# Second attention of a fused attention and GELU network: six more exps added on VectorE, GpSimd's squares regrouped, the last roots of batch 2 computed from SBUF

## The chip, the cores and the metric

The program runs on one core of one Trainium2 chip. The metric is the device time of one execution in microseconds (us), taken as the median of several executions. Five engines work beside each other, each on its own queue, in the order in which its instructions stand: PE (matrix products, TensorE), DVE (VectorE), ACT (ScalarE), POOL (GpSimd) and SP, which only issues transfers. An instruction that waits holds back everything behind it on its engine.

## What is computed

The reference is an attention over 8 batches and 12 heads (448 positions, 64 wide) with a root-mean-square norm on q and k, and a two-layer network on its result:

```python
def rmsnorm(x, g):
    rms = np.sqrt(np.mean(x * x, axis=-1, keepdims=True) + 1e-06)
    return x / rms * g
q_n, k_n = (rmsnorm(q, g_q), rmsnorm(k, g_k))
scores = scale * np.matmul(q_n, k_n.transpose(0, 1, 3, 2))
attn = np.exp(scores - max) / sum
x = attn @ v            # then regrouped to 3584 tokens x 768
h = x @ w_in            # 768 x 2048
out = gelu_tanh(h) @ w_out
```

## The kernel before

**Groups and batches.** The 12 heads of a batch are three groups of four, called c0, c1 and c2; (2, c1) means batch 2, group 1. Batch b runs in two stretches. In its *attention*, PE makes 21 score tiles ("units" u0 to u20, seven for each group, line 335); ACT takes the exp of each (line 343); then come for each group a product of the exps with a block of ones, which gives the sums (s0, s1, s2), and one with v (x0, x1, x2, both line 387). In its *first layer* (line 537) PE multiplies the result with `win`, and ACT applies GELU (line 543). The second layer of earlier batches (line 495) is cut in small rounds and put between the units of an attention. Batch 0 and the last second layer have code of their own.

**What sets the order.** Each attention has two strings: one for PE ("5r" is five rounds of the second layer, "u" a unit, "s" and "x" the two products) and one for DVE. The attention of batch 1 uses `SECOND`, those of batches 2 to 7 use `STEADY`. DVE's letters are: A, B, F, G add the seven exp tiles of a group (lines 355 to 362), so that the ones product needs few matmuls; T, R, S turn, invert and spread the sums (lines 397, 402, 409); M multiplies the x product with them into `xT` (line 422); E evicts a second-layer tile. Letters L, J, K and a0, a1, ... are places at which other work hangs. `added(b, c)` tells how many exps are added: a sum product over seven exp tiles is 7 x 4 matmuls, over one added tile 4.

**Preparing the next batch.** While batch 1 runs, batch 2 is prepared: q and k are loaded (SP), squared (ACT or POOL, line 164), summed over 64 columns (DVE, `total`, line 173), the inverse roots are made (ACT with Ln and Exp, line 198 and 205, or DVE with three Newton steps, `rsqrt_last`, lines 254 to 262), POOL multiplies (`normed`, line 278), SP transposes by DMA into `qT` and `kT` (line 319), and DVE multiplies `kT` with the gains (`gain`, line 325). A raw buffer is one of four per tag: the load of (3, c2) takes the buffer of (2, c1), so it goes out when POOL has normed (2, c1). On SP the first layer of batch 1 issues: the transposes of (2, c0), the loads of (3, c1), the transposes of (2, c1), the loads of (3, c2), the transposes of (2, c2). POOL then squares (3, c2), and DVE takes its two totals and the gain of (2, c2) at the start of the attention of batch 2, ahead of A0, its first addition.

**PSUM.** Four tiles of two banks (t0 to t3) go round: `pair(...)` gives the one that was given longest ago, whatever for, and its new writer waits for the old reader.

Of the kernel before, what the change touches and what calls it, by code (L numbers as in the profile page):

```python
# [8 lines left out]
F32 = mybir.dt.float32  # L9
# [8 lines left out]
def kernel(  # L18
# [224 lines left out]
    def rsqrt_last(b):  # L243


        c, flat, m = slice(NCH - 1, NCH), "p c n a t -> p (c n a t)", 4 * NT
        y, ms = rinvs[b][:, c].rearrange(flat), sss[b][:, c].rearrange(flat)
        if steady():
            own, dst = pair("root")[:, 0], y
        else:  # L250
            own, dst = oall[0][:, S:], place(b, 1)
        z, u = own[:, :m], own[:, m:2 * m]
        t = smp.tile([P, NCH * 4 * NT], F32, tag="lg", name="lg")[:, :m]
        nc.vector.tensor_scalar(u, ms, 1.0 / D, 1e-6, op0=ALU.mult, op1=ALU.add)
        nc.vector.tensor_scalar(
            y.bitcast(I32), u.bitcast(I32), -0.5, float(0x5F3759DF), op0=ALU.mult, op1=ALU.add
        )
        for i in range(3):
            nc.vector.tensor_copy(z, y)
            nc.vector.tensor_mul(t, z, y)  # L260
            nc.vector.scalar_tensor_tensor(z, t, -0.5, u, op0=ALU.mult, op1=ALU.mult)
# [85 lines left out]
    def added(b, c):  # L347

        return NT - 1 if b > 1 else (NT - 1, 0, NT - 2)[c] if b else 0
# [21 lines left out]
    def products(b, c, what, lo=0, hi=NT):  # L371
# [8 lines left out]
        if not what and added(b, c):  # L380
            es[:added(b, c) + 1] = [ess[b, c][:, 0]]
# [166 lines left out]
    def mm1_pair(i, cs=range(HP), b=0, js=range(2)):  # L548
# [29 lines left out]
        "3r u 5r uu 8r u 8r uu 8r u 5r u 4r u 7r us 4r u 4r u 3r uu 4r x 1r usu 3r u 6r u 2r u 5r"  # L578
        " uu 10r x 6r sx",
        "A0 L0 B0 F0 G0 J0 T0 R0 K0 S0 a0 a1 M0 T1 R1 S1 a2 A2 a3 B2 F2 M1 a4 a5 T2 R2 S2 M2",  # L580
        {6: 0, 14: 1, 21: 2},
    )

    def attention(b, side, extra, ends):
# [65 lines left out]
        for word in order.split():  # L650
# [5 lines left out]
            for w in word:  # L656
# [7 lines left out]
                else:  # L664
                    last = added(b, k)
                    assert {("u", t) for t in range(k * NT, (k + 1) * NT)} <= made
                    assert w == "x" or not last or ("FG"[last - NT + 2], k) in made
# [257 lines left out]
    for b in range(B):  # L925
        m1, side, extra, ends = [], [], [], []
        if b == 0:
# [85 lines left out]
        if b + 2 < B:  # L1013
            ends.append(lambda: rsqrt(b + 2, slice(0, NCH if b else NCH - 1)))
# [41 lines left out]
```

## Time and profile before

| | us |
|---|---|
| median of 3 executions | 391.45 (391.40 to 391.76) |
| the profiled execution | 391.23 |
| its span, first to last instruction | 389.2 |
| granted TensorE clock | 1.000 |
| attention of batch 1 on PE | 50.0 to 75.7 |
| first layer of batch 1 on PE | 75.7 to 94.35 |
| start of the attention of batch 2 | 94.35 |

A row of a timeline has the start in us from the start of the span, the time from the first start to the last end, engine, line, operation, out<-in and how many instructions; in brackets stands the idle time ahead of it and what ended it. Starts of rows are exact; a matmul's end is modelled, so the pace of PE is read from one row's start to the next.

### The profile page before, as it was taken

The page shows a single profiled execution, that of the slowest core. Times are in us where ns is not written, and L with a number is a line of the kernel's source. Part 1 is how long each engine was busy: PE and PEld are TensorE (multiplying, and loading weights), DVE is VectorE, ACT ScalarE, POOL GpSimd, SP SyncE. Part 2 cuts the span into 40 slices and gives each one's busy share as a digit, 9 for nine tenths or more (in the row PEclk, how much of TensorE's full clock was granted, in tenths as well). Part 3 has the DMA queues.
Part 4 walks back from the last instruction along what each step waited for, and adds up shares of the span by engine and source line. Part 5 has one row for each costly group of instructions (what it writes and reads, how often), then busy time and mean ns, then how long its engine had stood idle before and what let it go on. Part 6 is the DMA issues. An engine that isn't in the chain of part 4 may idle for free.

```text
span 389.2 us, 17542 instructions
## 1 busy us (share of the span) xinstructions
PE 380.6 (98%) x8060; PEld 294.0 (76%) x8060; DVE 235.9 (61%) x366; ACT 278.7 (72%) x353; POOL 126.3 (32%) x110
## 2 busy tenths in 40 slices
PE   7899999999999999999999999999999999999996
PEld 4565577877887788877888788877888778887664
DVE  5998938976596359836589257953598204980010
ACT  6995499767994689757995589946897449944300
POOL 5996506384005440093103740064300900000000
PEclk9999999999999999999999999999999999999999
DMA  8999999999614992379822995159631721120033
GB/s 266 322 231 211 210 230 263 223 200 264 113 44 100 243 213 58 80 132 217 194 65 65 214 227 103 45 110 251 108 80 50 125 44 42 44 65 4 2 83 81
DMA packets 64446, 54.68 MB, mean 141 GB/s; under 512 B 37620, under 2 KB 60020, under 8 KB 64372
## 3 DMA queue, kind: packets, MB, share of 16 engines
q1 hardware_dynamic: 53936, 41.33, 43.8%
q0 software_dynamic: 10128, 11.80, 18.5%
q8 instruction: 63, 1.03, 1.1%
q10 hardware_dynamic: 308, 0.43, 0.4%
q14 instruction: 11, 0.09, 0.1%
HBM read 45.61 MB, written 11.01 MB: 146 GB/s over the span
## 4 chain that ended last, share of the span: by engine, by line
PE 92%; ACT 5%; DMA 1%; issue 1%; DVE 0%; POOL 0%; DVEq 0%
PE t L537 33%; PE t L495 32%; PE t L387 9%; PE t L335 7%; PE t L463 5%; ACT ex L343 4%; PE t L556 4%; DMA rawq<-in_q_dram 1%; PE h L436 1%; PE tp L296 1%; PE o L387 0%; POOL nrmq L278 0%; ACT g L543 0%; DVE ss L173 0%; ACT sq L162 0%
## 5 line engine op out<-in xcount | busy, mean ns | idle before, releaser
L343 ACT ACTIVATE ex<-t,shift 128x896 bf16<-128x896 f32 x168 | 156.2, 1016 | 1.9 <-PE t L335 1.6
L495 PE MATMUL t<-wout,g 64*64 64x384 bf16 (+1 forms) x3456 | 150.6, 305 | 0.0
L537 PE MATMUL t<-xT,win 64*64 64x448 bf16 x2688 | 128.7, 349 | 0.3 <-ACT g L543 0.3
L495 PEld LDWEIGHTS <-g 64*64 64x64 bf16 x3456 | 112.9, 107 | 19.2
L537 PEld LDWEIGHTS <-win 64*64 64x64 bf16 x2688 | 96.6, 107 | 31.0 <-issue 0.5
L543 ACT ACTIVATE g<-t 128x896 bf16<-128x896 f32 x56 | 50.5, 915 | 57.1 <-PE t L537 57.1
L173 DVE TENSOR_REDUCE ss<-sq 128x14 f32<-128x896 f32 (+3 forms) x45 | 44.5, 997 | 51.9 <-ACT sq L162 49.1
L335 PE MATMUL t<-qT,kT 64*64 64x448 bf16 x672 | 58.2, 351 | 1.4 <-ACT ex L343 0.6
L799 POOL COPY mark<-es 1x1 bf16<-1x1 bf16 x7 | 1.2, 177 | 132.0 <-DVE es L362 128.3
L355 DVE TENSOR_TENSOR es<-ex 128x1792 bf16<-128x1792 bf16 x20 | 21.2, 1061 | 33.0 <-ACT ex L343 33.0
L278 POOL TENSOR_TENSOR nrmq<-rawq,rinv 128x896 bf16<-128x896 f32 (+1 forms) x21 | 34.9, 1660 | 18.6 <-ACT rinv L205 11.0
L278 POOL TENSOR_TENSOR nrmk<-rawk,rinv 128x896 bf16<-128x896 f32 (+1 forms) x21 | 34.4, 1640 | 0.0
L387 PE MATMUL t<-ex,vb 64*64 64x448 bf16 x588 | 31.9, 350 | 0.0
L335 PEld LDWEIGHTS <-kT 64*64 64x64 bf16 x672 | 25.5, 106 | 7.3 <-DVE kT L305 1.2
L397 DVE STREAM_TRANSPOSE st<-t 128x448 f32<-128x448 f32 x42 | 24.7, 626 | 9.7 <-PE t L387 9.7
L387 PEld LDWEIGHTS <-vb 64*64 64x64 bf16 x672 | 23.5, 107 | 7.3 <-issue 1.0
L409 DVE STREAM_TRANSPOSE rb<-rc 128x896 f32<-128x896 f32 (+1 forms) x25 | 26.7, 1068 | 0.3
L705 DVE COPY osb<-t 128x384 f32<-128x384 f32 (+1 forms) x4 | 2.0, 507 | 35.2 <-PE t L463 35.2
L422 DVE TENSOR_TENSOR xT<-t,rb 128x896 bf16<-128x896 f32 x21 | 22.8, 1087 | 0.8
L164 POOL TENSOR_TENSOR sq<-rawq 128x896 f32<-128x896 f32 (+1 forms) x9 | 13.6, 1513 | 28.6 <-DVE ss L173 27.3
L513 ACT COPY osb<-t 128x768 f32<-128x768 f32 (+1 forms) x18 | 12.6, 701 | 13.9 <-PE t L495 13.9
L358 DVE TENSOR_TENSOR es<-es,ex 128x1792 bf16<-128x1792 bf16 x20 | 21.3, 1063 | 0.7 <-ACT ex L343 0.6
(103 smaller groups left out, 313.5 us busy)
## 6 DMA issues: line engine op xcount, KB each, us to landing
rawq<-in_q_dram SPq DMA_DIRECT2D x22, 448.0 KB, 5.0
rawk<-in_k_dram SPq DMA_DIRECT2D x22, 448.0 KB, 5.8
out_dram<-osb SPq DMA_DIRECT2D x42, 192.0 KB, 2.7
vb<-in_v_dram POOLq DMA_DIRECT2D x6, 672.0 KB, 7.3
win<-in_moe_w_in_dram POOLq DMA_DIRECT2D x8, 384.0 KB, 10.8
wout<-in_moe_w_out_dram POOLq DMA_DIRECT2D x3, 768.0 KB, 17.1
out_dram<-osb SPq DMA_DIRECT2D x24, 96.0 KB, 3.7
vb<-in_v_dram POOLq DMA_DIRECT2D x2, 448.0 KB, 15.5
```

The lines of the kernel that those rows point to most:

```text
L173: nc.vector.reduce_sum(sss[b][:, seat(b, c), "qk".index(n), hs, ts], squares(b, c, n, hs, ts), axis=AX.X)
L278: eng.tensor_mul(nrms[n, b, c][:, ts].rearrange("p t a d -> p a t d"), raws[n, b, c][:, :, ts], root[:, :, ts].to_broadcast([P, 2, m, D]),)
L335: nc.tensor.matmul(sc[r * R:(r + 1) * R, a, :S], kT[rs, c, t, r], qT[b][rs, c, :, r], start=True, stop=True,)
L343: nc.scalar.activation(exs[b, c][:, t], scs.pop((b, c, t))[:, :, :S], AF.Exp, scale=scale, bias=shift)
L358: nc.vector.tensor_add(es, es, ex[:, 4:6])
L387: nc.tensor.matmul(o[r][a * D:(a + 1) * D], vb[b % 2][rs, 2 * c + a, i] if what else ones[rs], es[i][rs, a], start=(i == 0), stop=(i == n ...
L397: nc.vector.transpose(st[:, r].rearrange("p a b -> p (a b)"), o[r])
L409: nc.vector.transpose(oas["rb"][:, rs].rearrange("p r s -> p (r s)"), rc.to_broadcast([128, (rs.stop - rs.start) * m, 32]),)
L422: nc.vector.tensor_mul(xT[b][:, 2 * c:2 * c + 2], oas["o", c, 1][:, :, :S], oas["rb"])
L495: mm = nc.tensor.matmul(o[a * R:(a + 1) * R, bank, :hi - lo], g[rs, f, at:at + R], wout[rs, f, lo:hi], start=(n == 0), stop=(n == len(step ...
L537: mm = nc.tensor.matmul(h[a * R:(a + 1) * R, j, :S], win[rs, c, at:at + R], xT[b][rs, c], start=begin and c == cs[0], stop=end and c == cs ...
L543: nc.scalar.activation(g[:, 2 * i:2 * i + 2, (b % 2) * S:(b % 2 + 1) * S], h[:, :, :S], AF.Gelu_apprx_tanh,)
```

## The change

The line numbers in the diff's new code are not those of the profile. Parts of the diff that only rename are left out.

```diff
-    def rsqrt_last(b):
+    def rsqrt_last(b, c=slice(NCH - 1, NCH)):
-        c, flat, m = slice(NCH - 1, NCH), "p c n a t -> p (c n a t)", 4 * NT
+        flat, m = "p c n a t -> p (c n a t)", (c.stop - c.start) * 4 * NT
         y, ms = rinvs[b][:, c].rearrange(flat), sss[b][:, c].rearrange(flat)
         if steady():
-            own, dst = pair("root")[:, 0], y
+            own = consts.tile([P, 2, m], F32, name="zu")
+            z, u = own[:, 0], own[:, 1]
+            dst = y
...
     def added(b, c):
-        return NT - 1 if b > 1 else (NT - 1, 0, NT - 2)[c] if b else 0
+        return NT - 1 if b > 1 else (NT - 1, NT - 2, NT - 2)[c] if b else 0
...
         if not what and added(b, c):
-            es[:added(b, c) + 1] = [ess[b, c][:, 0]]
+            es[:added(b, c) + 1] = [ess[b, c][:, i] for i in range(1 + ((b, c) == (1, 1)))]
...
     SECOND = (
-        "3r u 5r uu 8r u 8r uu 8r u 5r u 4r u 7r us 4r u 4r u 3r uu 4r x 1r usu 3r u 6r u 2r u 5r"
-        " uu 10r x 6r sx",
-        "A0 L0 B0 F0 G0 J0 T0 R0 K0 S0 a0 a1 M0 T1 R1 S1 a2 A2 a3 B2 F2 M1 a4 a5 T2 R2 S2 M2",
-        {6: 0, 14: 1, 21: 2},
+        "5r u 1r u 2r u 6r u 9r u 1r u 5r u 6r u 8r u 5r su 3r u 6r u 4r u 3r uxu 5r u 4r"
+        " us 1r u 6r uu 2r u 9r x 5r sx",
+        "A0 L0 B0 F0 G0 J0 T0 R0 S0 A1 K0 B1 M0 a0 T1 R1 A2 S1 B2 F2 M1 a1 T2 R2 S2 M2",
+        {8: 0, 13: 1, 21: 2},
     )
...
-                      ("L0", lambda: late_loads(2, 1)), ("a1", lambda: late_loads(2, 2)),
+                      ("L0", lambda: late_loads(2, 1)), ("a0", lambda: late_loads(2, 2)),
...
-            extra += [("J0", lambda: gpsimd_waits(ess[1, 0][:1, 0, 0, :1])),
-                      ("K0", lambda: gpsimd_waits(kT[:1, 2, 0, 0, :1]))]
-            at = 0
-            for c in range(2):
-                for n in "qk":
-                    for hs in (slice(0, 1), slice(1, 2)) if c else (both,):
-                        extra += [
-                            ("K0" if at else "J0",
-                             lambda c=c, n=n, hs=hs: square(2, c, n, nc.gpsimd, hs)),
-                            (f"a{at}", lambda c=c, n=n, hs=hs: total(2, c, n, hs))]
-                        at += 1
+            extra.append(("J0", lambda: gpsimd_waits(ess[1, 0][:1, 0, 0, :1])))
+            for at, n in enumerate("qk"):
+                extra += [
+                    ("J0", lambda n=n: square(2, 0, n, nc.gpsimd)),
+                    (f"a{at}", lambda n=n: total(2, 0, n))]
         elif b + 1 < B:
             m1.append((0, lambda: gpsimd_waits(ess[b, NCH - 1][:1, 0, 0, :1])))
+            if b == 1:
+                halves = [(n, slice(a, a + 1)) for n in "qk" for a in range(2)]
+                m1 += [(0, lambda n=n, hs=hs: square(2, 1, n, nc.gpsimd, hs)) for n, hs in halves]
+                m1 += [(0, lambda n=n, hs=hs: total(2, 1, n, hs)) for n, hs in halves]
+                m1 += [(0, lambda n=n: total(2, 2, n)) for n in "qk"]
+                m1.append((0, lambda: rsqrt_last(2, slice(1, NCH))))
             for c in range(NCH):
-                if b == 1 and c + 1 == NCH:
-                    m1 += [(0, lambda: total(2, 2, "q")), (0, lambda: total(2, 2, "k")),
-                           (0, lambda: rsqrt_last(2))]
                 m1 += [(0, lambda c=c: normed_both(b + 1, c, nc.gpsimd)),
                        (4 * c + 4, lambda c=c: transposed(b + 1, c))]
-            m1 += [(9, lambda: gain(b + 1, 0)), (14, lambda: gain(b + 1, 1))]
+            m1.append((9, lambda: gain(b + 1, 0)))
+            if b == 1:
+                extra.append(("first", lambda: gain(2, 1)))
+            else:
+                m1.append((14, lambda: gain(b + 1, 1)))
...
-            ends.append(lambda: rsqrt(b + 2, slice(0, NCH if b else NCH - 1)))
+            ends.append(lambda: rsqrt(b + 2, slice(0, NCH if b else 1)))
```

So the exps of (1, c1) are added by A1 and B1 into two half sums, and s1 is 3 x 4 matmuls in place of 7 x 4. POOL squares (2, c0) in one go in the attention of batch 1, and (2, c1) after it. ACT makes the roots of (2, c0) alone; DVE's Newton steps make those of (2, c1) and (2, c2) together, 56 columns in place of 28, and take no PSUM tile.

How the instructions stand on DVE from M1 of batch 1 (xT, the first row) to the Newton steps, before and then now. `ss<-sq` are totals, 128x7 a half and 128x14 a whole one; the rows from L397 (now L398) on are T2, R2, S2, M2.

```order
L422 TENSOR_TENSOR xT<-t_100,rb 128x896
L173 TENSOR_REDUCE ss<-sq 128x7 x2
L397 STREAM_TRANSPOSE st<-t_893 128x448 x2
L402 RECIPROCAL rc<-st 128x28
L409 STREAM_TRANSPOSE rb<-rc 128x896
L422 TENSOR_TENSOR xT<-t_101,rb 128x896
L173 TENSOR_REDUCE ss<-sq 128x14 x2
L254 TENSOR_SCALAR t_101<-ss 128x28
L255 TENSOR_SCALAR rinv<-t_101 128x28
```

```order
L423 TENSOR_TENSOR xT<-t_101,rb 128x896
L173 TENSOR_REDUCE ss<-sq 128x14
L398 STREAM_TRANSPOSE st<-t_893 128x448 x2
L403 RECIPROCAL rc<-st 128x28
L410 STREAM_TRANSPOSE rb<-rc 128x896
L423 TENSOR_TENSOR xT<-t_100,rb 128x896
L173 TENSOR_REDUCE ss<-sq 128x7 x4
L173 TENSOR_REDUCE ss<-sq 128x14 x2
L255 TENSOR_SCALAR zu<-ss 128x56
L256 TENSOR_SCALAR rinv<-zu 128x56
```

The four half totals of (2, c1) now stand between M2 and the Newton steps, and one whole total in place of two halves stands between M1 and T2.

POOL over the same stretch, before and then now. `mark` is a copy of one element by which POOL waits for an addition on DVE (or for `kT`), `sq` are squares (128x896 a whole group, 128x448 half a group), `nrmq` and `nrmk` the norming of (2, c0), (2, c1) and (2, c2) in this order.

```order
L799 COPY mark<-es 1x1
L164 TENSOR_TENSOR sq<-rawq 128x896
L799 COPY mark<-kT 1x1
L164 TENSOR_TENSOR sq<-rawk 128x896
L164 TENSOR_TENSOR sq<-rawq 128x448 x2
L164 TENSOR_TENSOR sq<-rawk 128x448 x2
L147 DMA vb_121<-in_v_dram 128x6x448
L799 COPY mark<-es 1x1
L278 TENSOR_TENSOR nrmq<-rawq,rinv 128x2x7x64
L278 TENSOR_TENSOR nrmk<-rawk,rinv 128x2x7x64
```

```order
L801 COPY mark<-es 1x1
L164 TENSOR_TENSOR sq<-rawq 128x896
L164 TENSOR_TENSOR sq<-rawk 128x896
L147 DMA vb_121<-in_v_dram 128x6x448
L801 COPY mark<-es 1x1
L164 TENSOR_TENSOR sq<-rawq 128x448 x2
L164 TENSOR_TENSOR sq<-rawk 128x448 x2
L279 TENSOR_TENSOR nrmq<-rawq,rinv 128x2x7x64
L279 TENSOR_TENSOR nrmk<-rawk,rinv 128x2x7x64
```

The squares of (2, c1) moved behind the second mark, that is behind F2 of batch 1, and stand ahead of the first norming. Behind these rows the order on POOL is as before, and so is DVE's from the totals of batch 3 to A0 of batch 2:

```order
L173 TENSOR_REDUCE ss_1831<-sq_1942 128x14
L173 TENSOR_REDUCE ss_1831<-sq_1971 128x14
L326 TENSOR_SCALAR kT_124<-kT_124,gcols_113 128x896
L173 TENSOR_REDUCE ss_1831<-sq_2052 128x14
L173 TENSOR_REDUCE ss_1831<-sq_2054 128x14
L326 TENSOR_SCALAR kT_124<-kT_124,gcols_113 128x896
L356 TENSOR_TENSOR es_2210<-ex_2112 128x1792
L514 COPY osb_2249<-t1_101 128x768
```

These are (now, with the numbers of the buffers) the two totals of (3, c1), the gain of (2, c1), the two totals of (3, c2), the gain of (2, c2), then A0 and the eviction E0; none of them moved against the others. On SP, the eight stores of the first two evictions now stand together ahead of the loads of (2, c2), and the transposes and loads behind them are in the order of before.

More of the change, by code (lines that the diff above doesn't have):

```diff
@@ L241, in rsqrt_newton @@
             )
-    def rsqrt_last(b):
-        c, flat, m = slice(NCH - 1, NCH), "p c n a t -> p (c n a t)", 4 * NT
+    def rsqrt_last(b, c=slice(NCH - 1, NCH)):
+        flat, m = "p c n a t -> p (c n a t)", (c.stop - c.start) * 4 * NT
         y, ms = rinvs[b][:, c].rearrange(flat), sss[b][:, c].rearrange(flat)
         if steady():
-            own, dst = pair("root")[:, 0], y
-        else:
-            own, dst = oall[0][:, S:], place(b, 1)
-        z, u = own[:, :m], own[:, m:2 * m]
+            own = consts.tile([P, 2, m], F32, name="zu")
+            z, u = own[:, 0], own[:, 1]
+            dst = y
+        else:
+            z, u = oall[0][:, S:S + m], oall[0][:, S + m:S + 2 * m]
+            dst = place(b, 1)
         t = smp.tile([P, NCH * 4 * NT], F32, tag="lg", name="lg")[:, :m]
@@ L666, in attention @@
                     assert {("u", t) for t in range(k * NT, (k + 1) * NT)} <= made
-                    assert w == "x" or not last or ("FG"[last - NT + 2], k) in made
+                    assert w == "x" or not last or ("BG" if (b, k) == (1, 1) else "FG")[
+                        last - NT + 2] + str(k) in {x + str(i) for x, i in made}
                     products(b, k, "sx".index(w))
```

## The prediction

> **What bounds the kernel now.** I read the page's chain of waits first, then PE's timeline over the stretch that the change touches, then the other engines' timelines there.
>
> ```profile
> PE 92%; ACT 5%; DMA 1%; issue 1%; DVE 0%; POOL 0%; DVEq 0%
> ```
>
> PE makes 92% of the chain that ended last, so the time changes only by matmuls that go and by time in which PE stands. From the timeline of PE (attention of batch 1, its first layer, attention of batch 2):
>
> ```profile
> 65.05 1.52 PE L387 MATMUL t<-ex,ones 64*64 64x448 bf16 x28
> 75.73 6.63 PE L537 MATMUL t<-xT,win 64*64 64x448 bf16 x136
> 82.62 11.92 PE L537 MATMUL t<-xT,win 64*64 64x448 bf16 x248 [0.26 <-ACT g L543]
> 94.35 1.01 PE L495 MATMUL t<-wout,g 64*64 64x384 bf16 x20
> 102.66 0.39 PE L335 MATMUL t<-qT,kT 64*64 64x448 bf16 x4
> ```
>
> The 248 matmuls of the third row take 94.35 - 82.62 = 11.73 us. Four 64x64 ones run side by side, so that is 62 groups of 0.19 us. The 136 of the second row, 34 groups, should take 6.43 and take 82.62 - 75.73 = 6.89: PE stands 0.46 us there, and waits for ACT's GELU. The last row is u7 of batch 2. It needs the PSUM tile that E0 empties on DVE. From DVE's timeline (end of batch 1's attention, its first layer, start of batch 2's attention):
>
> ```profile
> 73.30 1.09 DVE L422 TENSOR_TENSOR xT<-t,rb 128x896 bf16<-128x896 f32 x1
> 74.31 1.14 DVE L173 TENSOR_REDUCE ss<-sq 128x7 f32<-128x448 f32 x2
> 75.36 1.17 DVE L397 STREAM_TRANSPOSE st<-t 128x448 f32<-128x448 f32 x2
> 78.17 1.09 DVE L422 TENSOR_TENSOR xT<-t,rb 128x896 bf16<-128x896 f32 x1
> 79.18 2.07 DVE L173 TENSOR_REDUCE ss<-sq 128x14 f32<-128x896 f32 x2
> 81.28 0.19 DVE L254 TENSOR_SCALAR t<-ss 128x28 f32<-128x28 f32 x1
> 95.55 1.08 DVE L173 TENSOR_REDUCE ss<-sq 128x14 f32<-128x896 f32 x1 [0.58 <-POOL sq L164]
> 96.55 0.44 DVE L325 TENSOR_SCALAR kT<-kT,gcols 128x896 bf16<-128x896 bf16 x1
> 100.56 1.09 DVE L355 TENSOR_TENSOR es<-ex 128x1792 bf16<-128x1792 bf16 x1 [3.56 <-ACT ex L343]
> 101.57 0.95 DVE L513 COPY osb<-t 128x768 f32<-128x768 f32 x1
> ```
>
> A0 of batch 2 starts at 100.56 and E0 ends at 102.52, 0.14 us ahead of u7. So PE goes straight through, but with next to nothing to spare. What covers it is the 3.56 us for which DVE had been idle before A0: the last total of batch 3 (95.55) and the last gain of batch 2 (96.55) were done early. That cover is what the change spends.
>
> **What goes.** s1 has 12 matmuls in place of 28: 4 groups of 0.19 less, 0.76 us. The Newton steps no longer take one of the four PSUM tiles in turn, so the fourth GELU pair gets the tile that M2 has freed, not the one whose GELU has just begun: the 0.46 us go. With nothing else PE would be 1.22 us earlier at the attention of batch 2. The two extra additions A1, B1 (about 1 us each on DVE) lie beside PE in an attention in which DVE waited several times; their cover is the wait for exps. The loads of (2, c2) go out a few us later behind the second eviction's stores, and by the landings below still land before ACT's squares of them; POOL's squares of (2, c1) must only be there before M2 ends. These three cost nothing.
>
> **What becomes late.** I follow one chain by its rows: DVE's end of attention, Newton, POOL's norming of (2, c1), SP, the load of (3, c2), POOL's squares, DVE's last total, the gain, A0, E0, u7. First, where M1 falls. ACT in the attention of batch 1, and the pitch of DVE's steps from an attention in which the order is A, S, B, F, M, as it now is:
>
> ```profile
> 51.55 5.50 ACT L343 ACTIVATE ex<-t,shift 128x896 bf16<-128x896 f32 x6
> 56.91 0.90 ACT L518 COPY osb<-t 128x384 f32<-128x384 f32 x2
> 57.64 7.36 ACT L343 ACTIVATE ex<-t,shift 128x896 bf16<-128x896 f32 x8
> 106.98 1.05 DVE L355 TENSOR_TENSOR es<-ex 128x1792 bf16<-128x1792 bf16 x1
> 107.94 1.10 DVE L409 STREAM_TRANSPOSE rb<-rc 128x896 f32<-128x896 f32 x1
> 108.97 1.05 DVE L358 TENSOR_TENSOR es<-es,ex 128x1792 bf16<-128x1792 bf16 x1
> 110.06 0.62 DVE L360 TENSOR_TENSOR es<-es 128x896 bf16<-128x896 bf16 x1
> 110.60 1.08 DVE L422 TENSOR_TENSOR xT<-t,rb 128x896 bf16<-128x896 f32 x1
> ```
>
> An exp takes (56.91 - 51.55) / 6 = 0.89 us of ACT, an eviction's two copies 0.73. Ahead of u17's exp stand 17 exps and two evictions: it starts at 51.55 + 15.2 + 1.5 = 68.2 if ACT never waits, and ends at 69.2. A2 follows, and S1, B2, F2, M1 at the pitches above (0.96, 1.03, 1.09, 0.54): M1 at 72.9. From M1 to M2 it was 78.17 - 73.30 = 4.87; a whole total (1.0) in place of two halves (1.05) makes 4.8: M2 at 77.7, the totals at 78.7. Now come four halves (two took 75.36 - 74.31 = 1.05, so 2.1) and the two whole ones (81.28 - 79.18 = 2.1): Newton starts at 82.9 against 81.28, though PE is earlier.
>
> The Newton steps themselves, 56 columns wide in SBUF. The groups of operations give the same instruction in both widths, and POOL's timeline what follows:
>
> ```profile
> L233 DVE SCALAR_TENSOR_TENSOR lg<-lg,ss 128x56 f32<-128x56 f32 x3 | 0.7, 217 | 0.1
> L261 DVE SCALAR_TENSOR_TENSOR t<-lg,t 128x28 f32<-128x28 f32 x3 | 0.6, 192 | 0.1
> 59.76 1.67 POOL L164 TENSOR_TENSOR sq<-rawq 128x896 f32<-128x896 f32 x1
> 84.50 1.69 POOL L278 TENSOR_TENSOR nrmq<-rawq,rinv 128x896 bf16<-128x896 f32 x1 [1.68 <-issue]
> 86.15 1.69 POOL L278 TENSOR_TENSOR nrmk<-rawk,rinv 128x896 bf16<-128x896 f32 x1
> 91.96 1.68 POOL L164 TENSOR_TENSOR sq<-rawq 128x896 f32<-128x896 f32 x1 [4.12 <-DVE ss L173]
> 93.70 1.82 POOL L164 TENSOR_TENSOR sq<-rawk 128x896 f32<-128x896 f32 x1
> ```
>
> From Newton's first operation to the norming behind it was 84.50 - 81.28 = 3.22; twelve of the fourteen operations are 25 ns longer, so 3.5. POOL norms q of (2, c1) at 86.4 and k at 88.05 (1.65 later), done at 89.75. Before, (2, c1) was normed ahead of the Newton steps; this is the one step that gets much later. The transfers of SP, and their times to landing in this stretch:
>
> ```profile
> 79.55 1.57 SPq L319 DMA_TRANSPOSE kT<-nrmk  x1
> 81.17 0.57 SPq L124 DMA_DIRECT2D rawq<-in_q_dram  x1
> 81.80 0.49 SPq L124 DMA_DIRECT2D rawk<-in_k_dram  x1
> 83.70 2.29 SPq L319 DMA_TRANSPOSE kT<-nrmk  x1
> 86.05 0.58 SPq L124 DMA_DIRECT2D rawq<-in_q_dram  x1
> rawq<-in_q_dram SPq DMA_DIRECT2D x3, 448.0 KB, 5.0
> rawk<-in_k_dram SPq DMA_DIRECT2D x3, 448.0 KB, 5.5
> kT<-nrmk SPq DMA_TRANSPOSE x3, 5.8
> ```
>
> SP is idle by then, so the transpose of k goes out at 89.8, the load of (3, c2)'s q 1.6 later (81.17 - 79.55) at 91.4, of k 0.6 after that at 92.05; they land at 96.4 and 97.55. Before, q went out at 86.05. POOL squares q at 96.45 and k 1.74 later (93.70 - 91.96), done at 100.0. DVE's last total follows at 100.05, the gain at 101.05, A0 at 101.45. The transpose that the gain needs goes out at about 94.6 and lands 5.8 later, at 100.4, just before. So A0 starts 0.89 us **later** than the 100.56 of before, though PE would let it start 1.2 us earlier. E0 follows at the same distance, u7 loses its spare 0.07 (0.14 less a wake-up of about 0.07), and the rest of the program hangs on u7. The sum: the gains of 1.22 go, and 0.89 - 0.07 = 0.8 us is lost. PE stands about 2 us ahead of u7. 391.23 + 0.8 = 392.0 for a profiled execution, and 0.2 more for the median (391.45 against 391.23): **392.3**.
>
> **Bounds.** Behind the second pair of transposes SP took 2.35 us to the next load (86.05 - 83.70) in place of 1.6; my DVE steps may be 0.3 out either way, and the landings 0.4. Late by all of it (0.75 + 0.3 + 0.4 less what POOL's squares of q leave idle) A0 starts at up to 102.9, a loss of 2.3; 102.5 and 1.9 if the landings hold. If SP issues the load within 1.3 and both land 0.4 sooner, with DVE 0.3 earlier, the squares of k start at 97.2 and A0 at 100.4: nothing lost, about 391.3. I take the middle, since it goes by the rows of this very stretch. This case's own range is 391.2 to 393.4.
>
> **The rivals.** (1) *The chain is hidden*: (2, c1) is normed early enough, or the squares of (3, c2) follow faster. Point from which it decides: A0 by 99.4 (100.56 less 1.22). It needs 2 us less than I count. For it speaks that everything in the attention of batch 1 fits on PE; against it, that each step of the chain is a plain row. Then 391.45 - 1.22 = 390.2.
>
> (2) *The load lands late.* One load of this stretch shows what that is:
>
> ```profile
> rawq<-in_q_dram SPq DMA_DIRECT2D x1, 448.0 KB, 8.2
> ```
>
> That one, the load of (3, c0), went out in the attention of batch 1, beside the stores of an eviction and POOL's load of v. With 8.2 for the q of (3, c2), q lands at 99.6, its squares and those of k end at 103.2, and A0 starts at 104.7: 4.1 us lost, 395.5. Against it: neither stores nor the load of v are near it now. PE would then stand for over 5 us. The page "TensorE: Matmul & The Clock Gate" of the Trainium skill (Part 1, the HAM clock gate) says that an idle window of about 3.4 us drops the array to half its clock until it has been busy as long; by that, the rival would cost some 1.7 us more, and the 2 us of my forecast nothing. The profile shows the granted clock at 1.000 throughout, and no idle time long enough to test it.
>
> (3) *The attention of batch 1 gets waits of its own.* DVE's margins there are small now: s0 stands right behind G0, u16 needs M0 to have read its tile, s2 needs F2. POOL's squares of (2, c0) run in one go from 59.76 to 63.1, across the start of A1, which I put at 62.7. The Trainium skill's page "SBUF — State Buffer" (Who interferes with whom) says that a DVE instruction with two SBUF inputs waits for a GpSimd one that reads SBUF; by that A1 starts 0.4 later, M0 ends at about 66.6, and u16 is held by a tenth or so. No row here shows such a wait. For the Newton operands, now in SBUF, the rule changes nothing: POOL is done with (2, c0) at about 80 by my count (four half squares from 73.1, two normings of 1.65) and waits for them. Each such wait is 0.1 to 0.4 us and also moves u17's exp, the head of my chain; with 0.3 in all: 392.6.
>
> **How the numbers follow.** A measurement of this kernel can tell about 0.2% (0.78 us) from no change, so faster is under 390.67 and slower over 392.23. My chain 0.60, of which 0.38 is over 392.23 and 0.22 within; hidden 0.22, faster; late landing 0.10, slower; waits in batch 1's attention 0.08, of which 0.06 slower. Faster 0.22, within 0.24, slower 0.54. The range reaches from rival (1) at its lower edge, 390.1, to the late end of my own case, 393.4; what is left out is rival (2) and the tails. The likeliest case alone: 391.2 to 393.4.
>
> **What would show it.** On PE: s1 with 12 matmuls; no wait for a GELU in the first layer of batch 1, which then starts at about 75.0 and ends at about 93.1; one idle of about 2 us ahead of u7 of batch 2, put down to DVE's eviction. On DVE: Newton from 82.9, the last total of batch 3 released by POOL's squares at about 100, A0 straight behind the gain with no idle that ends on an exp. On SP: the load of (3, c2) at about 91.4. I am wrong if A0 of batch 2 still waits for the exp of u3, or if PE shows over 0.5 us of idle in the attention of batch 1.

## The result and the profile after

| us | before | changed |
|---|---|---|
| median of 20 executions each, same chip | 391.65 (391.06 to 393.29) | 392.55 (391.34 to 394.80) |
| ratio to before, 95% interval | | 1.0021 (1.0012 to 1.0030) |
| profiled execution, its span | 391.23, 389.2 | 393.08, 391.1 |
| granted TensorE clock | 1.000 | 0.999 |

The change makes the kernel 0.9 us slower; 392.3 was forecast. In the changed profile the attention of batch 1 starts at 50.74 instead of 50.00, because of a start-up that differs from one execution to the next (50.24 in a second profile of the same kernel, after_again below); times are compared below by their distance from that start. The lines of the program are one further than before (L336 is the product of q and k that was L335).

The page's chain of waits of the changed kernel:

```profile
PE 84%; DVE 4%; ACT 4%; POOL 3%; DMA 3%; SPq 1%; issue 1%; DVEq 0%; POOLq 0%
```

Before, this chain was 92% PE, and DVE, POOL, transfers and SP together were 1% of it. Now these are 11%: the chain leaves PE in the attention of batch 1 and comes back at u7 of batch 2. PE's timeline there (s1 in its two parts, x1, the first layer, the start of the attention of batch 2, u7):

```profile
67.58 0.57 PE L388 MATMUL t<-es,ones 64*64 64x448 bf16 x8
67.96 0.39 PE L388 MATMUL t<-ex,ones 64*64 64x448 bf16 x4
71.87 1.99 PE L388 MATMUL t<-ex,vb 64*64 64x448 bf16 x28
73.51 0.99 PE L496 MATMUL t<-wout,g 64*64 64x384 bf16 x17
...
76.03 18.51 PE L538 MATMUL t<-xT,win 64*64 64x448 bf16 x384
94.25 1.10 PE L496 MATMUL t<-wout,g 64*64 64x384 bf16 x20
104.26 0.38 PE L336 MATMUL t<-qT,kT 64*64 64x448 bf16 x4 [1.42 <-DVE osb L514]
```

s1 is 12 matmuls, and the 384 matmuls of the first layer are one row with no wait for a GELU inside. But PE stands 1.42 us ahead of u7, for the eviction E0. And one row is too long: from the 28 matmuls of x1 to the next row it is 73.51 - 71.87 = 1.64 us. Before, the same 28 took 73.06 - 71.73 = 1.33:

```profile
71.73 1.52 PE L387 MATMUL t<-ex,vb 64*64 64x448 bf16 x28
73.06 1.17 PE L495 MATMUL t<-wout,g 64*64 64x384 bf16 x24
```

These 0.31 us come up again below. The windows of the two kernels by stage (attention of batch 1, its first layer, attention of batch 2; stage, its length, then PE's busy time), before and then changed, put numbers on it:

```profile
50.00:75.73 25.73, 25.73 (x594) 19.46 (x596) 19.06 (x37) 23.38 (x30) 8.23 (x10) 1.00 0.95 238
75.73:94.35 18.62, 18.36 (x392) 13.73 (x385) 13.39 (x28) 13.20 (x20) 12.30 (x8) 1.00 1.14 220
94.35:121.19 26.84, 26.84 (x699) 22.79 (x693) 20.87 (x29) 23.94 (x30) 2.17 (x3) 1.00 0.48 109
```

```profile
50.74:76.03 25.29, 25.17 (x579) 18.32 (x581) 18.98 (x35) 22.89 (x30) 6.01 (x7) 1.00 1.05 247
76.03:94.25 18.22, 18.22 (x392) 15.12 (x388) 16.37 (x30) 13.32 (x20) 12.14 (x9) 1.00 0.66 141
94.25:123.03 28.78, 27.33 (x700) 22.86 (x695) 21.67 (x30) 24.20 (x30) 4.32 (x4) 1.00 0.66 149
```

The first two stages win 0.44 and 0.40 us; the third loses 1.94. The sum is a loss of 1.10: u7 comes 0.86 later than before (104.26 - 50.74 against 102.66 - 50.00), and the rest of that attention adds 0.24. PE came to that attention 0.84 earlier, so by the pace of its rows it lost 0.84 + 0.86 = 1.70 us ahead of u7; the row names 1.42 of it, since a matmul's end is modelled. DVE's timeline shows why E0 is late (M2, the totals, Newton's first operation, then the gain of (2, c0), the two totals of (3, c2), the gain of (2, c2), A0 and E0):

```profile
78.72 1.09 DVE L423 TENSOR_TENSOR xT<-t,rb 128x896 bf16<-128x896 f32 x1
79.73 4.17 DVE L173 TENSOR_REDUCE ss<-sq 128x7 f32<-128x448 f32 x6
83.94 0.19 DVE L255 TENSOR_SCALAR zu<-ss 128x56 f32<-128x56 f32 x1
89.19 1.81 DVE L326 TENSOR_SCALAR kT<-kT,gcols 128x896 bf16<-128x896 bf16 x1
99.25 1.09 DVE L173 TENSOR_REDUCE ss<-sq 128x14 f32<-128x896 f32 x1 [4.25 <-POOL sq L164]
100.89 1.09 DVE L173 TENSOR_REDUCE ss<-sq 128x14 f32<-128x896 f32 x1 [0.55 <-POOL sq L164]
101.89 0.45 DVE L326 TENSOR_SCALAR kT<-kT,gcols 128x896 bf16<-128x896 bf16 x1
102.25 1.08 DVE L356 TENSOR_TENSOR es<-ex 128x1792 bf16<-128x1792 bf16 x1
103.25 0.95 DVE L514 COPY osb<-t 128x768 f32<-128x768 f32 x1
```

A0 no longer waits for an exp: it stands right behind the gain, and that behind a total that waits for POOL's squares. POOL and SP of the same stretch (the norming of (2, c1), the squares of (3, c2); the transpose of k of (2, c1), the load of (3, c2)):

```profile
87.42 1.69 POOL L279 TENSOR_TENSOR nrmq<-rawq,rinv 128x896 bf16<-128x896 f32 x1 [6.03 <-DVE rinv L263]
89.07 1.69 POOL L279 TENSOR_TENSOR nrmk<-rawk,rinv 128x896 bf16<-128x896 f32 x1
97.54 1.68 POOL L164 TENSOR_TENSOR sq<-rawq 128x896 f32<-128x896 f32 x1 [3.34 <-DMA rawq<-in_q_dram]
99.18 1.68 POOL L164 TENSOR_TENSOR sq<-rawk 128x896 f32<-128x896 f32 x1
```

```profile
90.78 2.49 SPq L320 DMA_TRANSPOSE kT<-nrmk  x1
93.33 0.58 SPq L124 DMA_DIRECT2D rawq<-in_q_dram  x1
93.95 0.46 SPq L124 DMA_DIRECT2D rawk<-in_k_dram  x1
```

POOL waits for Newton's last operation, SP for POOL, POOL for the load, DVE for POOL, PE for DVE: every link is the end of the one before.

### The profile page after: what moved, and what is told of

It reads as the page before. It is cut to its first block, busy times and chain, and to the rows that moved or that the text cites. A ratio compares the mean times of both kernels' runs of the same rounds, so it can differ in the third digit from the quotient of the medians.

```text
span 391.1 us, 17509 instructions
## 1 busy us (share of the span) xinstructions
PE 381.1 (97%) x8044; PEld 294.5 (75%) x8044; DVE 240.8 (62%) x368; ACT 278.6 (71%) x353; POOL 126.2 (32%) x109
## 3 DMA queue, kind: packets, MB, share of 16 engines
q8 instruction: 63, 1.03, 1.1%
## 4 chain that ended last, share of the span: by engine, by line
PE 84%; DVE 4%; ACT 4%; POOL 3%; DMA 3%; SPq 1%; issue 1%; DVEq 0%; POOLq 0%
PE t L496 30%; PE t L538 28%; PE t L388 8%; PE t L336 7%; PE t L464 5%; PE t L557 4%; ACT ex L344 4%; DMA rawq<-in_q_dram 3%; DVE ss L173 2%; POOL g L164 1%; POOL nrmq L279 1%; POOL sq L164 1%; PE h L437 1%; DVE xT L423 1%; PE o L388 0%
## 5 line engine op out<-in xcount | busy, mean ns | idle before, releaser
L538 PEld LDWEIGHTS <-win 64*64 64x64 bf16 x2688 | 98.0, 107 | 29.3
L336 PE MATMUL t<-qT,kT 64*64 64x448 bf16 x672 | 59.0, 351 | 3.6 <-DVE osb L514 1.4
L356 DVE TENSOR_TENSOR es<-ex 128x1792 bf16<-128x1792 bf16 x21 | 22.5, 1070 | 29.5 <-ACT ex L344 29.4
L336 PEld LDWEIGHTS <-kT 64*64 64x64 bf16 x672 | 26.1, 106 | 10.2 <-issue 3.0
L398 DVE STREAM_TRANSPOSE st<-t 128x448 f32<-128x448 f32 x42 | 24.7, 627 | 9.5 <-PE t L388 8.6
L359 DVE TENSOR_TENSOR es<-es,ex 128x1792 bf16<-128x1792 bf16 x21 | 22.3, 1062 | 0.6 <-ACT ex L344 0.6
```

The source lines that it names most:

```text
L336: nc.tensor.matmul(sc[r * R:(r + 1) * R, a, :S], kT[rs, c, t, r], qT[b][rs, c, :, r], start=True, stop=True,)
L356: nc.vector.tensor_add(es, ex[:, :2], ex[:, 2:4])
L398: nc.vector.transpose(st[:, r].rearrange("p a b -> p (a b)"), o[r])
L538: mm = nc.tensor.matmul(h[a * R:(a + 1) * R, j, :S], win[rs, c, at:at + R], xT[b][rs, c], start=begin and c == cs[0], stop=end and c == cs ...
```

## The experiments

Each was timed beside the kernel before on one chip (medians of before: 391.41, 391.39 and 391.30 in the three sets). The table gives for each profile the lengths of the three stages, counted from the first matmul of each on PE, as in the windows above, and their sum's distance from before's 71.19. The last column is explained under "A stall that was not forecast"; its times are counted from the start of the span.

| kernel | median, ratio (95%) | att. 1 | layer 1 | att. 2 | sum to before | wait at u7 | fetch at, PE goes on |
|---|---|---|---|---|---|---|---|
| before | 1 | 25.73 | 18.62 | 26.84 | 0 | none | 68.2, no stall |
| changed | 392.55, 1.0021 (1.0012-1.0030) | 25.29 | 18.22 | 28.78 | +1.10 | 1.42 | 70.4, 72.9 |
| after_again | 392.46, 1.0025 (1.0011-1.0038) | 26.04 | 18.50 | 27.87 | +1.22 | 0.50 | 70.6, 73.16 |
| operands_psum | 392.90, 1.0031 (1.0019-1.0043) | 25.42 | 18.76 | 28.09 | +1.08 | 0.81 | 69.6, 72.18 |
| seven_again | 392.64, 1.0031 (1.0015-1.0047) | 26.97 | 18.19 | 27.80 | +1.77 | 0.66 | 71.0, 73.18 |
| totals_split | 391.44, 0.9991 (0.9973-1.0009) | 25.55 | 18.49 | 26.93 | -0.22 | none | 69.8, 72.27 |
| totals_later | 392.56, 1.0026 (1.0009-1.0042) | 26.11 | 18.49 | 27.02 | +0.43 | none | 70.4, 72.83 |
| sbuf_alone | 390.98, 0.9993 (0.9981-1.0004) | 25.73 | 18.16 | 26.83 | -0.47 | none | 68.4, no stall |
| one_total_more | 393.33, 1.0049 (1.0035-1.0064) | 25.76 | 18.22 | 28.85 | +1.64 | 1.72 | 69.8, 72.45 |
| split_late3 | 391.14, 0.9995 (0.9986-1.0005) | 26.13 | 18.49 | 26.93 | +0.36 | none | 70.4, 72.76 |
| split_early | 390.50, 0.9978 (0.9966-0.9990) | 24.96 | 18.16 | 27.05 | -1.02 | none | 69.2, no stall |
| after_early | 391.78, 1.0003 (0.9986-1.0019) | 24.95 | 18.16 | 28.83 | +0.75 | 1.72 | 69.2, no stall |
| split_vearly | 391.21, 0.9994 (0.9970-1.0017) | 25.29 | 18.16 | 26.84 | -0.90 | none | 67.6, no stall |

**Undoing one part.** If u7 is held by DVE's chain, the two gains on PE are worth nothing, and giving one of them back costs nothing. operands_psum puts Newton's operands back into one of the four PSUM tiles, with the width of the change:

```diff
-            own = consts.tile([P, 2, m], F32, name="zu")
-            z, u = own[:, 0], own[:, 1]
+            own = pair("root")[:, 0]
+            z, u = own[:, :m], own[:, m:2 * m]
```

> The changed kernel, but the Newton steps' operands lie in a PSUM tile out of the round again, 56 columns wide. Theory: the wait for a GELU in the first layer of batch 1 is back (0.3 to 0.5 us), but A0 of batch 2 starts at the same time, so the wait ahead of u7 is shorter by as much and the time is that of the changed kernel within 0.3 us (0.6 to 1.2 over the kernel before). Rival (each part is worth what it saves by itself): 0.46 us more, 1.2 to 1.5 over the kernel before.

The wait for a GELU is back, and the wait at u7 is shorter. Two rows of its PE timeline:

```profile
82.33 11.92 PE L538 MATMUL t<-xT,win 64*64 64x448 bf16 x248 [0.26 <-ACT g L544]
103.38 0.38 PE L336 MATMUL t<-qT,kT 64*64 64x448 bf16 x4 [0.81 <-DVE osb L514]
```

The first layer is 0.54 us longer than in the changed kernel and the attention behind it 0.69 shorter; the sums (+1.08 and +1.10) agree, and u7 comes 53.50 us behind the attention's start, where the changed kernel has 53.52. So in these two profiles the gain of the layer had gone into the wait. The medians alone don't settle it: operands_psum is 1.49 over before in its set, which is the rival's 1.2 to 1.5, but 1.21 by its ratio, and its interval overlaps with that of the changed kernel. seven_again takes A1 and B1 out and leaves s1 at 28 matmuls:

```diff
-        return NT - 1 if b > 1 else (NT - 1, NT - 2, NT - 2)[c] if b else 0
+        return NT - 1 if b > 1 else (NT - 1, 0, NT - 2)[c] if b else 0
...
-        "A0 L0 B0 F0 G0 J0 T0 R0 S0 A1 K0 B1 M0 a0 T1 R1 A2 S1 B2 F2 M1 a1 T2 R2 S2 M2",
+        "A0 L0 B0 F0 G0 J0 T0 R0 S0 K0 M0 a0 T1 R1 A2 S1 B2 F2 M1 a1 T2 R2 S2 M2",
```

> The changed kernel, but without A1 and B1: s1 is 28 matmuls over the seven exp tiles again. Theory: PE does 0.76 us more in the attention of batch 1 and the wait ahead of u7 is shorter by nearly as much, since DVE's last steps there hang on the exps of the third group, which come up to 0.4 us later: 0.7 to 1.4 us over the kernel before. Rival (each part is worth what it saves by itself): 1.4 to 1.8 over the kernel before.

The attention of batch 1 is 1.68 us longer (0.76 are the 16 matmuls, and 0.75 of the rest is the stall told of below), the attention of batch 2 is 0.98 shorter. This profile's sum is 0.67 over that of the changed kernel, and u7 comes 0.90 later (54.42 against 53.52). M1, the head of the chain, waits for x1 on PE here and starts 1.66 later than in the changed kernel (its DVE timeline):

```profile
74.90 1.09 DVE L423 TENSOR_TENSOR xT<-t,rb 128x896 bf16<-128x896 f32 x1 [1.21 <-PE t L388]
```

Both the stall and the 16 matmuls stand ahead of x1, and one profile can't part them. The stall alone is not enough: after_again has one of 0.90 and a sum of only +1.22. The medians differ by 0.09 (392.64 and 392.55), and the interval, 1.0015 to 1.0047, holds the theory as well as its rival. So whether the gain of s1 is worth nothing in the changed kernel is not shown.

**Taking the chain away from A0.** totals_split leaves all of the change and moves two steps of DVE behind A0 of batch 2: the gain of (2, c2), needed only for u14, and the second total of (3, c2), which keeps no buffer.

```diff
+        if b == 2:
+            dve = dve.replace("G0 T0", "G0 K0 T0").replace("G1 T1", "G1 a0 T1")
...
-                extra.append(("first", lambda n=n: total(b + 2, 2, n)))
+                extra.append(("a0" if b == 1 and n == "k" else "first",
+                              lambda n=n: total(b + 2, 2, n)))
...
-            extra.append(("first", lambda: gain(b + 1, 2)))
+            extra.append(("K0" if b == 1 else "first", lambda: gain(b + 1, 2)))
```

> The changed kernel, but in batch 2's attention the gain of (2, c2) stands between G0 and T0 and the total of (3, c2)'s k between G1 and T1; only the total of q stays ahead of A0. Theory (the late load of (3, c2) holds A0, and A0 holds u7 through E0): A0 starts within 0.4 us of the exp of u3's end, the wait for E0 ahead of u7 falls from 1.4 us to under 0.3, and the time is 0.4 to 0.9 us under the kernel before (about 390.8 on its 391.45). Rival (the loss comes from elsewhere, such as ports shared by DVE and POOL or the new order in the attention of batch 1): no faster than the changed kernel, 0.7 to 1.1 us over the kernel before.

A row of its DVE timeline, A0:

```profile
100.18 1.09 DVE L356 TENSOR_TENSOR es<-ex 128x1792 bf16<-128x1792 bf16 x1 [1.45 <-ACT ex L344]
```

A0 waits for an exp again, u7 for nothing, and the attention of batch 2 has its old length (26.93 against 26.84). That is worth about 1 us: 0.9991 in place of 1.0021 and 1.0025, with intervals that do not overlap. The time itself was a miss: 0.4 to 0.9 us under before was expected, and the medians (391.44 and 391.41) show no gain. It doesn't bring the whole 1.22, since the sum is only 0.22 below before. The missing 0.9 us are in the two earlier stages (25.55 and 18.49 where 24.97 and 18.16 were due). totals_later moves both totals, further back (q behind G1, k behind M1) and the gain behind R0:

> The changed kernel, but in batch 2's attention the gain of (2, c2) stands behind R0, the total of (3, c2)'s q between G1 and T1 and that of k between M1 and T2; nothing of the late chain stands ahead of A0. Theory: no wait ahead of u7; A0 waits for the exp of u3 again; up to 0.5 us comes back at the end of that attention, where M2 is a whole total later (its slack there is about 0.5 us): 0.2 to 0.9 us under the kernel before. Rival: as the changed kernel, 0.7 to 1.1 us over the kernel before.

The wait at u7 is gone here too, but the time was a miss: 1.0026, 1.0 to 1.2 us over before, where 0.2 to 0.9 under was expected. Two things make up most of it. The attention of batch 1 is 0.56 us longer than in totals_split, for nothing that the edit touches; it is the stall told of below. And behind the three stages of the table PE waits twice for DVE in the first layer of batch 2 (rows with 0.21 for a transposed sum and 0.24 for an `xT`), which takes 18.99 us in place of 18.16. So moving the totals that far back costs at the other end about what it saves at u7.

**Each half of the theory by itself.** sbuf_alone is the kernel before with Newton's operands in SBUF and nothing else:

```diff
-            own, dst = pair("root")[:, 0], y
+            own, dst = consts.tile([P, 2 * m], F32, name="zu"), y
```

> The kernel before with one part of the change alone: the operands of the last Newton steps in SBUF. Theory: the wait for a GELU in the first layer of batch 1 (0.46 us) goes; DVE's A0 of batch 2 still waits for an exp of ACT, which comes earlier with PE, so u7 loses none of it: about 391.0 against 391.4, ratio 0.9988, no wait at u7. Rival: the SBUF operands cost as much on DVE, or PE, being earlier, meets another wait at u7: 391.4, ratio 1.000.

In its profile the first layer takes 18.16 us in place of 18.62, so the forecast 0.46 are there and reach the end (sum -0.47). The medians differ by 0.41, but the interval, 0.9981 to 1.0004, doesn't exclude no change. one_total_more is the changed kernel with one total ahead of the Newton steps taken twice:

```diff
-                m1 += [(0, lambda n=n: total(2, 2, n)) for n in "qk"]
+                m1 += [(0, lambda n=n: total(2, 2, n)) for n in "qkk"]
```

> The changed kernel with one whole total (of k of (2, c2)) taken twice ahead of the Newton steps, so DVE is 1.05 us later there and nothing else is touched. Theory: the chain Newton, norming of (2, c1), load of (3, c2), its squares, its last total, A0, E0, u7 has no slack, so A0 and u7 come 1.0 us later, the wait at u7 grows from 1.4 to about 2.4 us, and the time is 393.6, ratio 1.0055 against before. Rival: u7 is held by something else, or the load or the transposes have slack: 392.6, ratio 1.003, wait unchanged.

It costs 0.8 to 1.0 us: it is 1.94 over before in its set, the changed kernel 0.90 and 1.16 in its two. Its interval lies above that of the first of these and just touches that of the second. And u7 starts 54.29 us behind the attention's start in place of 53.52:

```profile
104.10 0.38 PE L336 MATMUL t<-qT,kT 64*64 64x448 bf16 x4 [1.72 <-DVE osb L514]
```

So most of a us put on DVE ahead of Newton does come out at the end of the program, 20 us and four engines later. Not all of it, and the wait at u7 grew to 1.72, not to the expected 2.4: Newton began 1.59 later than in the changed kernel (1.05 for the total, most of the rest for a larger stall ahead of M1), but SP's transpose of k took 1.22 us here, where the changed kernel had 2.49, and the load went out only 0.32 later.

**A stall that was not forecast.** Eight of the thirteen profiles show a stall of PE in x1 of batch 1, or just ahead of it, for 0.25 to 1.06 us. The profile puts it down to "issue": PE waits for nothing that the profile shows. In the changed kernel the row of x1 hides it, and the weight loads of the same matmuls show it (PE's weight loads); then the rows of after_again, which is the changed kernel unaltered, and of split_late3:

```profile
72.91 0.52 PEld L388 LDWEIGHTS <-vb 64*64 64x64 bf16 x15 [0.55 <-issue]
```

```profile
73.16 0.95 PE L388 MATMUL t<-ex,vb 64*64 64x448 bf16 x15 [0.90 <-issue]
```

```profile
72.76 0.95 PE L388 MATMUL t<-ex,vb 64*64 64x448 bf16 x15 [0.96 <-issue]
```

It is always the same instruction: the 14th of x1's 28 matmuls, and in seven_again, where s1 has 16 more, 16 earlier. The page counts 63 packets of "instruction" traffic with 1.03 MB, so 16 KB each, on the same 16 DMA engines as the loads. Windows of 0.2 us over the DMA view find one such packet at about 70 us in each kernel, as in the changed kernel between 70.4 and 70.6:

```profile
q8 instruction: 1, 0.02, 27.5%
```

The last column of the table sets that window's start beside the time at which PE goes on. In all eight stalled profiles PE goes on 2.2 to 2.7 us behind the packet; where the packet came by 69.2, PE had no stall. Counted from the attention's start the two sorts part as well: up to 19.3 us no stall, from 19.7 a stall. Nor does PE come to the place at another time: in seven of the stalled profiles (all but seven_again) and in two without a stall (split_early, after_early) x1 begins 21.11 to 21.14 us behind the attention's start. What makes the packet late? In the change the loads of (2, c2) stand behind eight stores and go out together with those of (3, c0) at 68 to 71 us, and POOL, done sooner with its squares, sends the load of v (672 KB) at 63.8, not 68.8. split_late3 is totals_split with the loads of (3, c0) five units later, split_early with those of (2, c2) ahead of the stores:

```diff
-                side.append((3, lambda: loads(b + 3, 0)) if b else (14, lambda: late_loads(3, 0)))
+                side.append((3, lambda: loads(b + 3, 0)) if b else (19, lambda: late_loads(3, 0)))
```

```diff
-                      ("L0", lambda: late_loads(2, 1)), ("a0", lambda: late_loads(2, 2)),
+                      ("L0", lambda: late_loads(2, 1)), ("L0", lambda: late_loads(2, 2)),
```

> The version with the totals split (gain of (2, c2) and one total of (3, c2) behind A0) and, besides, the load of (3, c0) five units later, so that it no longer follows the load of (2, c2) at once. Theory A: the time in which PE has no instruction in x1 of batch 1 (0.25 to 1.06 us in five profiles) is an instruction fetch that is late behind the burst of two loads; it goes, and the time is about 391.0, ratio 0.999 or less, the row of 13 and 15 matmuls becoming one of 28. Theory B: it belongs to that place in PE's instructions whatever the transfers do: the idle time stays at 0.3 to 1.0 us, and the time is that of the split version, 391.4, ratio 1.000.

> The version with the totals split and, besides, the loads of (2, c2) out with those of (2, c1), ahead of the eight stores. Theory A (late fetch behind a burst of loads): about 0.9 MB less is under way when the fetch goes out, the idle time in x1 of batch 1 goes or shrinks under 0.2 us, and the time is about 391.0, ratio 0.999. Theory B (place alone): idle time and time as in the split version, 391.4. Rival to both: the mark in the buffer of (2, c2) waits for GpSimd on DVE ahead of B0 and delays s0, so PE shows new idle time before 60 us and the time is over 391.6.

split_late3 was a miss for the first theory as it stood there: the loads of (3, c0) go out at 71.29, behind the packet, and the stall is still 0.96. split_early is a hit: the packet at 69.2, no stall, x1 whole (its PE timeline):

```profile
71.14 1.52 PE L388 MATMUL t<-ex,vb 64*64 64x448 bf16 x28
```

A profile is one execution, and the stall differs between executions of one kernel (0.31 and 0.90 in the two profiles of the changed one), so the medians carry the verdicts. Both early stages now have the length that the prediction gave them, and this version beats both kernels: 390.50, 0.9978 (0.9966 to 0.9990) of before. after_early makes that one edit without the split of the totals, split_vearly leaves the loads where the change has them and sends the load of v earlier:

```diff
-            side += [(0 if b else 11, lambda: load_v(b + 2, 0, HP))]
+            side += [(0 if b else 5, lambda: load_v(b + 2, 0, HP))]
```

> The changed kernel unaltered, to have a second profile of it and a time on the same chip as the two others. 392.5, ratio 1.002; the wait at u7 about 1.4 us; the idle time of PE in x1 of batch 1 again there, 0.3 to 1.0 us, with PE going on 2.2 to 2.7 us behind the packet of instructions that the DMA engines carry at about 70 us (operands_psum 69.6 and 72.18, totals_split 69.8 and 72.27, the changed kernel 70.4 and 72.91, seven_again 71.0 and 73.18).

> The changed kernel with the loads of (2, c2) ahead of the eight stores alone, without the split of the totals. Theory: the idle time in x1 of batch 1 (0.3 us in the profile of the changed kernel) goes and M1, the head of DVE's chain, comes that much earlier, so u7 comes at most 0.3 to 0.6 us earlier but is still held by E0: 392.1, ratio 1.0015, wait at u7 over 1 us, attention of batch 1 shorter by 0.7 us than before's. Rival: the early loads alone do what split_early did, and the split of the totals was not needed: 390.6, ratio 0.998, no wait at u7.

> The version with the totals split, its loads of (2, c2) behind the stores as in the change, but GpSimd's load of v (672 KB in short packets) issued at the start of the attention of batch 1 instead of at about 63 us. Theory A: it was the load of v, which fills the DMA engines from 64 to 74 us since the change (before it went out at 68.8), that holds up the packet of instructions; the packet comes by 69.3 us, the idle time in x1 goes, 390.7, ratio 0.998. Theory B: the loads of (2, c2) alone hold it up: packet at 69.6 or later, idle time 0.3 to 1.0 us, 391.4, ratio 1.000. A third outcome, that the early load of v delays the loads of (2, c0) and so the squares and additions, would show as new idle time of PE before 68 us and over 391.6.

after_again gives the time of the changed kernel again, with a larger stall, a second one of about 0.3 us in the first layer, and a wait at u7 that is smaller by as much; its expected 1.4 us was off for that reason. The stall also moved M1 back by 0.76, but SP's transpose of k was shorter (1.84 us), and the load of (3, c2) went out only 0.11 later. The second stall, from its timeline of PE's weight loads:

```profile
79.36 15.28 PEld L538 LDWEIGHTS <-win 64*64 64x64 bf16 x327 [0.51 <-issue]
```

The four profiles with 18.49 or 18.50 us in the first layer all have this row, at the same 327 loads before the end; what makes it come in these four was not followed up.

after_early has the shortest attention and first layer of all, and the longest wait at u7, 1.72 us. That is the whole story in one profile: PE wins 1.24 us in two stages and gives 1.99 back in the third. Its median lies between those of before and of the changed kernel, and between theory and rival, and its interval overlaps with that of the changed kernel. split_vearly has its packet at 67.6 and no stall, though the loads of (2, c2) are late as in the change. So it was enough to take away either of the two, the load of v (in this one profile) or the loads of (2, c2) (in two), and the first theory fits in a wider form than it was put: what makes the packet late is all that stands ahead of it on the DMA engines, not one pair of loads. The median of split_vearly, 391.21 with an interval of 0.9970 to 1.0017, settles nothing, and its 390.7 was not met; its profile has the sum -0.90.

split_vearly showed one thing more. Its load of v, out at 44.68, delays k of (2, c0), and with it POOL's squares, across the start of A1: the third outcome of its expectation in small, with the units between x0 and s1 late and 0.33 us lost, though the median is not over 391.6. POOL's squares of k and DVE's A1, first in split_early, then in split_vearly:

```profile
61.42 1.67 POOL L164 TENSOR_TENSOR sq<-rawk 128x896 f32<-128x896 f32 x1
62.79 1.25 DVE L356 TENSOR_TENSOR es<-ex 128x1792 bf16<-128x1792 bf16 x1
```

```profile
61.79 1.67 POOL L164 TENSOR_TENSOR sq<-rawk 128x896 f32<-128x896 f32 x1 [0.41 <-DMA rawk<-in_k_dram]
62.72 1.69 DVE L356 TENSOR_TENSOR es<-ex 128x1792 bf16<-128x1792 bf16 x1
```

In both A1 ends 0.95 us behind POOL's squares, whenever it was begun.

## Why the prediction was right

The forecast was the likeliest case, the chain, with 392.3; 392.55 came. The path was right step by step; that the number came so close is in part luck, as the third point below says. Its steps, with the measured times less the 0.74 us of the later start:

| step | forecast | measured |
|---|---|---|
| attention of batch 1 on PE | -0.76 | -0.44 |
| first layer of batch 1 | -0.46 | -0.40 |
| M1, M2 | 72.9, 77.7 | 73.16, 77.98 |
| Newton's first operation | 82.9 | 83.20 |
| POOL norms (2, c1), q | 86.4 | 86.68 |
| SP: transpose of k | 89.8 | 90.04 |
| SP: load of (3, c2), q | 91.4 | 92.59 |
| POOL squares q, k | 96.45, 98.2 | 96.80, 98.44 |
| last total, gain, A0 | 100.05, 101.05, 101.45 | 100.15, 101.15, 101.51 |
| u7 against before | +0.82 | +0.86 |

- **The gains are there and reach nothing.** The profiles of sbuf_alone and split_early show both at their forecast size (-0.46 and -0.77); that of operands_psum shows that in the changed kernel the layer's gain goes into the wait at u7. For the gain of s1 seven_again leaves it open. The forecast of some 2 us in which PE stands ahead of u7 was 1.70 by PE's pace, since PE came 0.84 earlier and not 1.22. The attention won only 0.44 in the changed profile: "with nothing else PE would be 1.22 us earlier" left out the late packet of instructions. The prediction said that later loads of (2, c2) cost nothing. With the chain in charge that is not shown: after_early, whose loads go out early, is 0.68 under after_again in the same set, with intervals that overlap, and 0.35 to 0.47 under the changed kernel in the sums of the profiles. Once the chain is cut, they cost what totals_split lacks against split_early, 0.8 us in the profiles.
- **The chain is the bound.** Taking it from A0 (totals_split) removes the wait at u7; lengthening it by one total (one_total_more) adds to the time. It has some give all the same: what SP's transposes take (next point) moved the load by up to 1.3 us from run to run.
- **Two terms were mis-sized and nearly cancelled.** The transpose of k held SP longer than counted (2.55 us to the next load where 1.6 was taken), and with it and the 0.24 from the steps ahead the load was 1.2 late; it then landed in about 4.2 us, not 5.0. The upper bound of the prediction had taken the slow issue, its lower one the fast landing; that they met in one execution, so that A0 was only 0.06 off, is luck. M2 and the Newton steps were 0.3 late, about 0.1 of it by the stall in x1.
- **Rival (3), waits in the attention of batch 1,** was real, as an extra and not in place of the chain: A1 did not start 0.4 later, as the prediction worked out for this rival, but at 62.78 (less the later start); it took 1.25 us beside POOL's squares, and 1.69 in split_vearly. On the page "SBUF — State Buffer" of the Trainium skill (Who interferes with whom) a VectorE instruction with two SBUF inputs contends with a GpSimd one that reads SBUF; the traces agree, with 1.03 to 1.09 us for the same addition when POOL is idle. The prediction's 0.1 to 0.4 us for such a wait fit; the larger delay in that stage, the fetch, was not on the list. The sign that would have made the prediction wrong, over 0.5 us of idle PE in that attention, stands in after_again (0.90), and the time is the same: that idle time shortened the wait at u7, and what it added to the head of the chain (0.76 us at M1) SP's faster issue took back.
- **Rivals (1) and (2)** did not happen: A0 came at 101.51 where hiding needed 99.4, and the load landed in 4.2 us where rival (2) had 8.2.
- **The idle PE kept its clock.** The Trainium skill's "TensorE: Matmul & The Clock Gate" (Part 1, the HAM clock gate) lets the clock drop after some 3.4 us of idling; idle times of up to 1.72 us here left it at 0.998 to 1.000. No idle time here was as long as the page's.

The remaining 0.24 us of loss behind u7 were in no step of the sum. Some 0.2 of it lie right ahead of the unit that starts at 108.75 in the changed profile, where the profile names no releaser; no run was made for it.

## What to carry to other kernels

A gain on the bounding engine counts only up to the next instruction at which that engine waits for another: look for the smallest spare time downstream (here 0.14 us at u7), ask what holds it, and follow that chain back past loads and buffers for as far as it goes; here it began 30 us earlier. When such a chain has to become longer, reorder its end first: two DVE steps moved behind A0 were worth about 1 us, though the same steps moved further back cost it again. And when transfers are regrouped, the engines' own instruction traffic stands in the same line.

## What the hardware showed

- **Instruction fetch can stop PE.** With the DMA engines busy from 64 us on, a 16 KB packet of instructions came at 69.6 to 71.0 us in place of 67.6 to 69.2, and PE stood for 0.25 to 1.06 us at one fixed instruction, without a releaser in the profile. The Trainium skill's "Runtime: NRT & Kernel Launch" (Instruction fetch mechanics) calls the cost of such a block mostly hidden; in eight of thirteen profiles here it was not. That the packet is late because of the transfers ahead of it is what two edits that moved only transfers speak for, in three profiles; when the packet was asked for, no profile shows.
- **A plain gain took 1.81 us instead of 0.45.** DVE's gain of (2, c0) in the changed kernel began at 89.19, 0.12 behind the start of POOL's norming of k, and ended 0.24 behind its end. It lay off the path this time, since DVE then waited for POOL anyway.
- **SP's issue of one transpose** took between 1.22 and 2.55 us, on the same line and with the same shape. What sets it stayed open; it moves the next load by as much.
